# Joining values and scores of the first twelve attention trios, beginning the weights beside them, and spreading the later blocks

## The chip, the cores and the metric

The kernel runs on one core of a Trainium2 chip. The metric is the device time of one execution in microseconds (us); the profile of one execution gives the time of every instruction on the engines: TensorE (PE, matmuls; PEld its weight loads), VectorE (DVE), ScalarE (ACT), GpSimd (POOL) and SyncE (SP, which issues most DMAs).

## What is computed

Windowed attention over 8 batches and 8 heads of 576 positions (64 values a head), then a feed-forward layer on the 4608 x 512 result.

```python
scores = scale * np.matmul(q, k.transpose(0, 1, 3, 2))
mask_plain = (rel >= 0) & (rel < window)                                   # heads 0 to 3, window 32
mask_dil = (rel >= 0) & (rel < window * dilation) & (rel % dilation == 0)  # heads 4 to 7, dilation 4
attn = softmax(np.where(masks, scores, -1e9))
x = (attn @ v).transpose(0, 2, 1, 3).reshape(4608, 512)
h = x @ w_in                                   # 512 x 2048
g = h * np.clip(h + 3.0, 0.0, 6.0) / 6.0
out = g @ w_out                                # 2048 x 512
```

## The kernel before

**Attention.** The work is cut into 48 trios: a trio is one third of a batch's positions for four heads, in 12 query blocks of 32 positions and two pairs of heads. A trio's steps are: 24 small matmuls for the scores (`mm_scores`, 64 rows by 32 columns of the array each), softmax on VectorE and ScalarE (`softmax`: max L186, subtract L187, exp L191, and for later trios the mask added at L184), a turn of e (`st_turn_e`), 24 small matmuls for the values (`mm_values_first` or `mm_values`), the division by the row sums (`normalise`: z L198, reciprocal L199, x L201), a turn of x (`st_turn_x`), and the split of x into a rounded high part xh (ScalarE, L300) and the rest xl (GpSimd, L303). A small matmul of f32 data is two passes in the profile. The array has eight tiles of 64 x 32; scores use four of them, values four.

The first 12 trios (`NFIRST`) turn e and x on TensorE (`turn`, L243, with copies to SBUF on ScalarE at L246 and L248) and add their mask by a matmul (L215). The later ones turn by blocks on VectorE and by small DMAs (`turn_by_blocks`, L262 to L266), and their values of trio t and scores of trio t+1 are issued alternately as one block (`st_both`).

**Feed-forward.** The 4608 rows are cut into 12 chunks of 384. A step is a pair (chunk c, part f of 16). `gemm1` runs 12 matmuls of 384 columns into a PSUM buffer ps_h, of which there are two; each product is made of three, high by high, low by high and high by low part. ScalarE (L413, L417) and VectorE (L414, L418) make t, gh and gl of it; L414 frees ps_h. `gemm2` runs 9 matmuls of 512 columns into three ps_o buffers, two steps behind `gemm1`. Chunk 0 needs trios 0 to 4, chunk 1 also trios 5 to 9, and so on; chunk 3 needs trio 16.

**Weights.** Each of the 32 half parts of the weights is loaded as 64-bit words by one DMA (`load_w`) and converted in beats: `cv_fields` (ScalarE multiplies L339 and L340, VectorE shift L341), `cv_join` (VectorE and-or L347 and add L351, a custom instruction; ScalarE cast L352), `cv_split` (VectorE subtract L356). Part f needs half parts 2f and 2f+1.

**Order.** Each engine runs its instructions in a fixed order. A scheduler makes it from priorities that the program sets by `turn_of`, and from its own timeline. In the front, the first 15 rounds (tau), `first_items` gives the steps of the first trios; `LD`, `CB` and `EARLY` name the rounds in which a weight is loaded, a conversion beat is run, and a step of the feed-forward is begun; `BASE` and `CD` shift their priorities. `LEAD` steps of chunk 0 go ahead, then chunks 0 and 1 alternate. From chunk 2 on, the list `at` places the later attention blocks beside half steps (a step has two halves).

Of the kernel before, what the change touches and what calls it, by code (L numbers as in the profile page):

```python
# [8 lines left out]
F32 = mybir.dt.float32  # L9
# [9 lines left out]
P = 128  # L19
QB = 32  # L20
DIL = 4
RT = 3
TB = 4 * RT
SPARE = 2
WORK = 11
BEATS = 30  
CB = (6, 7, 8, 8, 10, 11)  
EXTRA = 2  
PRIO = -500
WARM = 8    # L30
ONV = ()
AHEAD = 1  
AHEAD0 = 2  
LD = (2, 3, 4, 6, 14)  
NFIRST = 12
FIRST0, FIRST1 = 5, 4
AT0, AT1 = 1, 8
NLOAD = 3
BASE = 13  
CD = 2    # L40
EARLY = (9, 11, 12, 12, 13)  
DEL = 0.2  
G2 = 0.8  
EV = -1.9  
NEG = -1.0e30


# [1 line left out]
def windowed_attention_ffn(ctx: ExitStack, tc: tile.TileContext, qk, vp, w, mask, out):  # L49
# [100 lines left out]
    def mm_scores(t, ps, i, u, r, masked):  # L150

        x, rows = kqs[t], slice(r * D, (r + 1) * D)
        n, kb, at = SLOTS * u + i, (SLOTS + 1) * u + i, QB * (2 * r + u)
        last["pe"] = nc.tensor.matmul(  # L154
            ps[at : at + QB, 2 * QB * i : 2 * QB * (i + 1)],
            lhsT=x[rows, KW + QB * n : KW + QB * (n + 1)], rhs=x[rows, QB * kb : QB * (kb + 2)],
            start=not masked, stop=(i == SLOTS - 1 or not masked),
        )

    def mm_values_first(t, ps, i, u, h):  # L160

        k, j = divmod(i, 2)
        rows, n, at, s = slice(j * D, (j + 1) * D), 4 * k + 2 * h + u, QB * (2 * u + j), 2 * k + h
        last["pe"] = nc.tensor.matmul(  # L164
            ps[at : at + QB, s * W : (s + 1) * W],
            lhsT=ats[t][rows, QB * n : QB * (n + 1)], rhs=vs[t][rows, n, :], start=True, stop=True,
        )

    def mm_values(t, ps, i, u, r):

        rows, n, at = slice(r * D, (r + 1) * D), SLOTS * u + i, QB * (2 * (1 - r) + u)
        last["pe"] = nc.tensor.matmul(  # L172
            ps[at : at + QB, i * W : (i + 1) * W],
            lhsT=ats[t][rows, QB * n : QB * (n + 1)], rhs=vs[t][rows, n, :], start=True, stop=True,
        )

    def softmax(t, ps, masked):
        e = work_tile("e")
        mx = small.tile([P, SLOTS], F32, name="mx")
# [6 lines left out]
        nc.vector.tensor_reduce(out=mx, in_=sv, axis=AX.X, op=ALU.max)  # L186
        nc.vector.tensor_tensor(  # L187
            out=ev, in0=sv, in1=mx.rearrange("p (s o) -> p s o", o=1).broadcast_to([P, SLOTS, 2 * QB]),
            op=ALU.subtract,
        )  # L190
        nc.scalar.activation(e, e, AF.Exp, scale=SCALE)  # L191
        es[t] = e
        load_qk(t + NLOAD)

    def normalise(t, ps):
        pv = ps[:, : SLOTS * W].rearrange("p (s x) -> p s x", x=W)
        z = small.tile([P, SLOTS], F32, name="z")
        nc.vector.tensor_scalar_add(z, pv[:, :, D], 1e-9)  # L198
        nc.vector.reciprocal(z, z)  # L199
        x = work_tile("x")  # L200
        nc.vector.tensor_tensor(  # L201
            out=x.rearrange("p (s x) -> p s x", x=D), in0=pv[:, :, 0:D],
            in1=z.rearrange("p (s o) -> p s o", o=1).broadcast_to([P, SLOTS, D]),
            op=ALU.mult,
        )
# [6 lines left out]
    def st_scores_first(t):  # L212
        ps = ps_a.tile([P, 512], F32, name="ps_a")
        _, kind, part = trios[t]
        nc.tensor.matmul(ps[:, :CH], lhsT=ident_b, rhs=mask_sb[:, 3 * kind + part], start=True, stop=False)  # L215
        for i, u, r in blocks():
            mm_scores(t, ps, i, u, r, True)
        softmax(t, ps, True)

    def st_values_first(t):  # L220
        ps = ps_a.tile([P, 512], F32, name="ps_a")
        for i, u, r in blocks():
            mm_values_first(t, ps, i, u, r)
        normalise(t, ps)

    def st_both(ts, tv):

        ps = ps_a.tile([P, 512], F32, name="ps_a") if ts is not None else None
        pv = ps_a.tile([P, 512], F32, name="ps_a") if tv is not None else None
        for i, u, r in blocks():  # L230
            if tv is not None:
                mm_values(tv, pv, i, u, r)
            if ts is not None:
                mm_scores(ts, ps, i, u, r, False)
        if tv is not None:
            normalise(tv, pv)
        if ts is not None:
            softmax(ts, ps, False)

    def turn(src, name):  # L240
        ps = ps_a.tile([P, 512], F32, name="ps_a")
        for r in range(RT):
            nc.tensor.transpose(ps[:, r * P : (r + 1) * P], src[:, r * P : (r + 1) * P], ident)  # L243
        dst = work_tile(name)
        if name == "a":
            nc.scalar.copy(dst, ps[:, :CH])  # L246
        else:
            nc.scalar.copy(  # L248
                dst.rearrange("p (u k x) -> p k u x", u=2, k=RT),
                ps[:, :CH].rearrange("p (k u x) -> p k u x", u=2, k=RT),  # L250
            )
        return dst

# [117 lines left out]
    def convert_beat():  # L371
        if beat["split"] < beat["join"]:
            cv_split(beat["split"])
            beat["split"] += 1
        if beat["join"] < beat["fields"]:
            cv_join(beat["join"])
            beat["join"] += 1
        p = beat["fields"]
        if p < NP:
            load_ahead(p + 1)  # L380
            if p < beat["loaded"]:
                cv_fields(p)
                beat["fields"] += 1
        load_ahead(p + (AHEAD if "g" in last else AHEAD0))

    def weights_ready(f):
        while beat["split"] < 2 * (f + 1):
# [74 lines left out]
    place = lambda p, step: beside.setdefault(halves[p], []).append(step)  # L462
    place(at[0] - FIRST1, lambda: st_both(NFIRST, None))
    place(at[0] - FIRST1 + 2, lambda: st_turn_e(NFIRST, turn_by_blocks))
    for i, p in enumerate(at):
        t = NFIRST + i
        more = t + 1 < T
        place(p, lambda t=t, more=more: st_both(t + 1 if more else None, t))
        place(p + 1, lambda t=t: st_turn_x(t, turn_by_blocks))
        if more:  # L470
            place(p + 2, lambda t=t: st_turn_e(t + 1, turn_by_blocks))
        place(p + 3, lambda t=t: st_split(t))

    def step_at(n):
        c, f = steps[n] if n < len(steps) else (None, None)
        turn_of(n)
# [12 lines left out]
        for step in beside.get((c, f, 1), []):  # L489
            step()  # L490
        turn_of(n + 0.9)
        if n < BEATS and n % EXTRA == 0:
            convert_beat()

    first[0] = BASE * STEP
# [8 lines left out]
    n = 0  # L504
    for tau in range(NFIRST + 3):
        turn_of(tau - BASE)
        for step, t in first_items(tau):
            step(t)
        turn_of(tau - BASE + CD)
        load_ahead(LD.count(tau) + beat["loaded"])  # L510
# [100 lines left out]
```

## Time and profile before

| | us |
|---|---|
| median of 3 runs | 922.7 |
| fastest run | 922.14 |
| the profiled execution | 923.19 |
| its span, first to last instruction | 921.4 |
| mean granted TensorE clock | 0.988 |

The third of the runs, at 4496.82 us, is an outlier and is left out of the argument. The profile comes from one execution. An instruction's row has its start and duration, engine, line, operation, what it writes and reads, and in brackets how long the engine had been idle before it and what ended that. A window's row has busy times, not progress: a busy TensorE may be running at half clock, which the granted clock tells (1.00 is full speed).

### The profile page before, as it was taken

Reading aid. Unit: us, or ns where it says so; the run is one execution under the profiler, and the core shown is the slowest. Engines: PE = TensorE matmul, PEld = TensorE weight load, DVE = VectorE, ACT = ScalarE, POOL = GpSimd, SP = SyncE. Lnnn points to the kernel's source line nnn. Section 1 sums busy time; section 2 is a strip of 40 time slices with the busy share of each in tenths; the row PEclk is TensorE's granted clock in tenths of the full one; section 3 lists DMA queues with packets and bytes.
Section 4 is the critical chain, followed back from the end, with each engine's and each line's share of the span. In section 5 each row is a group of like instructions: output and inputs, shape, how many; then the busy total and the mean of one; then the engine's idle time right before and its main releaser. Section 6 shows DMA issues by size and latency. Waiting matters only on the chain.

```text
span 921.4 us, 20615 instructions
## 1 busy us (share of the span) xinstructions
PE 892.1 (97%) x8732; PEld 795.2 (86%) x8732; DVE 447.5 (49%) x934; ACT 348.1 (38%) x661; POOL 58.9 (6%) x77
## 2 busy tenths in 40 slices
PE   7789999999889999999999999999999999999997
PEld 4569999988778998989899888989988998899996
DVE  3778878534544544544454454445444444422221
ACT  3767666532224333234233333323333332322322
POOL 0211000000010000001000100000000010000000
PEclk9999999999899999999999999999999999999999
DMA  9756233023222212212222122112212210100000
GB/s 326 252 182 260 78 92 92 24 92 90 87 88 93 75 52 82 82 48 86 56 72 85 49 82 82 53 58 81 74 48 82 84 33 10 43 5 1 35 1 34
DMA packets 37676, 74.87 MB, mean 81 GB/s; under 512 B 7248, under 2 KB 16464, under 8 KB 37584
## 3 DMA queue, kind: packets, MB, share of 16 engines
q1 hardware_dynamic: 32400, 64.12, 21.8%
q10 hardware_dynamic: 5184, 9.44, 2.8%
q8 instruction: 68, 1.11, 0.5%
q14 instruction: 24, 0.20, 0.1%
HBM read 57.02 MB, written 9.44 MB: 72 GB/s over the span
## 4 chain that ended last, share of the span: by engine, by line
PE 93%; DVE 3%; DMA 2%; ACT 1%; issue 0%; SPq 0%; DVEq 0%
PE ps_o L429 15%; PE ps_h L408 15%; PE ps_h L409 14%; PE ps_h L410 14%; PE ps_o L430 14%; PE ps_o L431 14%; PE ps_a L172 3%; PE ps_a L154 2%; DMA st<-in_w 1%; DMA kq<-in_qk 1%; PE ps_a L243 1%; DVE x L201 1%; PE ps_a L164 1%; DVE st L347 1%; DMA mi<-in_mask 1%
## 5 line engine op out<-in xcount | busy, mean ns | idle before, releaser
L408 PE MATMUL ps_h<-xh,wt 128*128 128x384 f32 x768 | 261.3, 340 | 7.2 <-DVE t L414 7.2
L409 PE MATMUL ps_h<-xl,wt 128*128 128x384 f32 x768 | 260.3, 339 | 0.0
L410 PE MATMUL ps_h<-xh,wt 128*128 128x384 f32 x768 | 260.1, 339 | 0.0
L414 DVE SCALAR_TENSOR_TENSOR t<-t,ps_h 128x384 f32<-128x384 f32 x192 | 106.0, 552 | 297.7 <-ACT t L413 277.5
L429 PE MATMUL ps_o<-wt,gh 128*128 128x512 f32 x576 | 228.9, 398 | 0.0
L430 PE MATMUL ps_o<-wt,gh 128*128 128x512 f32 x576 | 225.4, 391 | 0.0
L431 PE MATMUL ps_o<-wt,gl 128*128 128x512 f32 x576 | 221.5, 391 | 0.0
L413 ACT ACTIVATE t<-ps_h,three 128x384 f32<-128x384 f32 x192 | 111.5, 581 | 246.7 <-PE ps_h L410 240.7
L408 PEld LDWEIGHTS ps_h<-xh,wt 128*128 128x128 f32 x768 | 145.4, 189 | 16.2 <-DVE t L414 8.9
L418 DVE TENSOR_TENSOR gl<-t,gh 128x384 fp32r<-128x384 f32 x192 | 107.3, 559 | 95.2 <-ACT gh L417 95.1
L409 PEld LDWEIGHTS ps_h<-xl,wt 128*128 128x128 f32 x768 | 145.6, 190 | 7.5
L417 ACT CAST gh<-t 128x384 fp32r<-128x384 f32 x192 | 98.4, 513 | 136.2 <-DVE t L414 131.9
L410 PEld LDWEIGHTS ps_h<-xh,wt 128*128 128x128 f32 x768 | 146.0, 190 | 0.2
L431 PEld LDWEIGHTS ps_o<-wt,gl 128*128 128x128 f32 x576 | 108.2, 188 | 23.0
L429 PEld LDWEIGHTS ps_o<-wt,gh 128*128 128x128 f32 x576 | 109.1, 189 | 17.8
L430 PEld LDWEIGHTS ps_o<-wt,gh 128*128 128x128 f32 x576 | 108.9, 189 | 15.7
L303 POOL TENSOR_TENSOR xl<-xf,xh 128x384 fp32r<-128x384 f32 (+3 forms) x72 | 58.6, 825 | 752.2 <-ACT xh L300 751.5
L191 ACT ACTIVATE e<-e 128x384 f32<-128x384 f32 x48 | 25.2, 526 | 101.9 <-DVE e L187 101.7
L154 PE MATMUL ps_a<-kq 64*32 64x64 f32 x2304 | 54.6, 226 | 4.7 <-issue 3.6
L300 ACT CAST xh<-xf 128x384 fp32r<-128x384 f32 (+3 forms) x72 | 33.6, 533 | 48.9 <-DMA xf<-xf_t 48.7
L154 PEld LDWEIGHTS ps_a<-kq 64*32 64x32 f32 x2304 | 44.6, 107 | 8.7 <-issue 7.2
L172 PEld LDWEIGHTS ps_a<-v,a 64*32 64x32 f32 x1728 | 36.1, 105 | 10.7 <-issue 10.7
(41 smaller groups left out, 458.4 us busy)
## 6 DMA issues: line engine op xcount, KB each, us to landing
kq<-in_qk SPq DMA_DIRECT2D x48, 416.0 KB, 4.6
v<-in_v SPq DMA_DIRECT2D x48, 390.0 KB, 3.7
st<-in_w SPq DMA_DIRECT2D x32, 512.0 KB, 5.1
out<-o ACTq DMA_DIRECT2D x36, 256.0 KB, 2.1
a<-a_t SPq DMA_DIRECT2D x144, 24.0 KB, 1.8
xf<-xf_t SPq DMA_DIRECT2D x144, 24.0 KB, 1.8
mi<-in_mask SPq DMA_DIRECT2D x1, 608.0 KB, 4.6
```

The source lines that it names most:

```text
L154: last["pe"] = nc.tensor.matmul(ps[at : at + QB, 2 * QB * i : 2 * QB * (i + 1)], lhsT=x[rows, KW + QB * n : KW + QB * (n + 1)], rhs=x[rows ...
L172: last["pe"] = nc.tensor.matmul(ps[at : at + QB, i * W : (i + 1) * W], lhsT=ats[t][rows, QB * n : QB * (n + 1)], rhs=vs[t][rows, n, :], st ...
L408: nc.tensor.matmul(ph, lhsT=wt[f][:, 0, ks], rhs=a, start=(kt == 0), stop=False)
L409: nc.tensor.matmul(ph, lhsT=wt[f][:, 0, ks], rhs=b, start=False, stop=False)
L410: last["pe"] = nc.tensor.matmul(ph, lhsT=wt[f][:, 1, ks], rhs=a, start=False, stop=(kt == NK - 1))
L413: nc.scalar.activation(t, ph, AF.Relu, bias=three, scale=1.0)
L414: nc.vector.scalar_tensor_tensor(out=t, in0=t, scalar=6.0, in1=ph, op0=ALU.min, op1=ALU.mult)
L417: nc.scalar.copy(gh, t)
L418: nc.vector.tensor_tensor(out=gl, in0=t, in1=gh.bitcast(F32), op=ALU.subtract)
L429: nc.tensor.matmul(po[c][tt], lhsT=gh[:, ts], rhs=wt[f][:, 2], start=(f == 0), stop=False)
L430: nc.tensor.matmul(po[c][tt], lhsT=gh[:, ts], rhs=wt[f][:, 3], start=False, stop=False)
L431: last["pe"] = nc.tensor.matmul(po[c][tt], lhsT=gl[:, ts], rhs=wt[f][:, 2], start=False, stop=(f == NF - 1))
```

## The change

The first 12 trios go through `st_both` too: values of trio tau-2 and scores of trio tau are issued alternately, values on the four tiles that the scores leave free, so the array positions of both are exchanged. The turns of e (trio tau-1) and of x (trio tau-3) stand ahead of that block in a round. Weights are loaded one per round from round 2 and converted from round 4 on, one to two beats a round; the steps begin in round 8, when five trios are done, with four steps of chunk 0 ahead. The blocks of the later trios, from chunk 2 on, are 19/3 halves apart for the first ten and 8 halves after that (4 for the first six and 8 before), begin five halves before chunk 2, and split x one half later.

```diff
-CB = (6, 7, 8, 8, 10, 11)
-AHEAD = 1
-AHEAD0 = 2
-LD = (2, 3, 4, 6, 14)
-FIRST0, FIRST1 = 5, 4
-AT0, AT1 = 1, 8
-BASE = 13
-CD = 2
-EARLY = (9, 11, 12, 12, 13)
+AHEAD = 2
+LEAD = 4
+LD = (2, 3, 4, 5, 6, 7, 8, 9, 10, 11, 12, 13)
+CB = (4, 5, 6, 6, 7, 7, 8, 8, 9, 9, 10, 10, 11, 11)
+BASE = 8
+CD = 0.5
+EARLY = (8, 9, 10, 11, 12, 13, 13)
...
-    LEAD = 2
...
     def mm_scores(t, ps, i, u, r, masked):
-        n, kb, at = SLOTS * u + i, (SLOTS + 1) * u + i, QB * (2 * r + u)
+        h = r if t < NFIRST else 1 - r
+        n, kb, at = SLOTS * u + i, (SLOTS + 1) * u + i, QB * (2 * (1 - h) + u)
...
     def st_both(ts, tv):
+        masked = ts is not None and ts < NFIRST
+        if masked:
+            _, kind, part = trios[ts]
+            nc.tensor.matmul(ps[:, :CH], lhsT=ident_b, rhs=mask_sb[:, 3 * kind + part], start=True, stop=False)
         for i, u, r in blocks():
             if tv is not None:
-                mm_values(tv, pv, i, u, r)
+                (mm_values_first if tv < NFIRST else mm_values)(tv, pv, i, u, r)
             if ts is not None:
-                mm_scores(ts, ps, i, u, r, False)
+                mm_scores(ts, ps, i, u, r, masked)
...
     def first_items(tau):
-        todo = []
-        for lag, step in ((0, st_scores_first), (1, lambda t: st_turn_e(t, turn)), (2, st_values_first),
-                          (3, lambda t: st_turn_x(t, turn)), (3, st_split)):
-            if 0 <= tau - lag < NFIRST:
-                todo.append((step, tau - lag))
-        return todo
+        some = lambda t: t if 0 <= t < NFIRST else None
+        if some(tau - 1) is not None:
+            st_turn_e(tau - 1, turn)
+        if some(tau - 3) is not None:
+            st_turn_x(tau - 3, turn)
+            st_split(tau - 3)
+        if some(tau) is not None or some(tau - 2) is not None:
+            st_both(some(tau), some(tau - 2))
...
-    at = [FIRST0 + FIRST1 * i for i in range(6)]
-    at += [2 * NF * c + AT0 + AT1 * i for c in range(1, NCH) for i in range(4)]
-    at = at[: T - NFIRST]
+    at = [1 + 19 * i // 3 for i in range(10)]
+    at += [at[-1] + 8 * (i + 1) for i in range(T - NFIRST - 10)]
...
-        place(p + 3, lambda t=t: st_split(t))
+        place(p + 4, lambda t=t: st_split(t))
...
-        if n < BEATS:
+        if LEAD <= n < BEATS:
             convert_beat()
```

Further edits follow from these: the row positions in `mm_values_first`, the copy of the turned x (L248), and `load_ahead` at the head of a round.

What the scheduler makes of it is seen in the orders. Names with a number are single buffers. The first place is the front on TensorE, one round of the first trios; here the rows of the kernel before (L154 scores, L164 values, L243 turns, L215 mask).

```order
L215 MATMUL ps_a_252<-mi_78 128x384
L154 MATMUL ps_a_252<-kq_138 32x64 x24
L243 MATMUL ps_a_285<-ident_79,e_205 128x128 x3
L164 MATMUL ps_a_291<-v_103,a_216 32x65 x24
L243 MATMUL ps_a_323<-ident_79,x_246 128x128 x3
```

And of the changed kernel, from the end of one block to the beginning of the next (L151 scores, L161 values, L230 turns, L216 mask, L395 and L396 a piece of `gemm1`).

```order
L161 MATMUL ps_a_350<-v_105,a_258 32x65
L151 MATMUL ps_a_349<-kq_177 32x64
L395 MATMUL ps_h_803<-xh_76,wt_414 128x384
L396 MATMUL ps_h_803<-xl_77,wt_414 128x384
L230 MATMUL ps_a_420<-ident_79,e_407 128x128 x3
L230 MATMUL ps_a_426<-ident_79,x_403 128x128 x3
L216 LDWEIGHTS mi_78
L216 MATMUL ps_a_436<-mi_78 128x384
L161 MATMUL ps_a_437<-v_243,a_339 32x65
L151 MATMUL ps_a_436<-kq_250 32x64
```

Both turns and a piece of `gemm1` now stand between two blocks; before, the scores of a trio stood ahead of the turn of the trio before it. The second place is ScalarE in the same rounds: before (L191 exp, L339 and L340 multiplies, L246 and L248 copies of the turned e and x, L300 cast to xh).

```order
L246 COPY a_619<-ps_a_615 128x384
L191 ACTIVATE e_608<-e_608 128x384
L339 ACTIVATE st_331<-st_331 128x512
L340 ACTIVATE st_331<-st_331 128x512
L352 CAST wt_578<-st_331 128x512
L248 COPY xf_657<-ps_a_653 128x3x2x64
L300 CAST xh_76<-xf_657 128x2x48
L300 CAST xh_76<-xf_657 128x2x144
```

And in the changed kernel (L188 exp, L326 and L327 multiplies, L233 and L235 copies, L287 cast, L339 now the cast of a weight).

```order
L188 ACTIVATE e_407<-e_407 128x384
L233 COPY a_424<-ps_a_420 128x384
L235 COPY xf_430<-ps_a_426 128x6x2x32
L287 CAST xh_76<-xf_430 128x2x144
L287 CAST xh_76<-xf_430 128x2x48
L326 ACTIVATE st_252<-st_252 128x512
L327 ACTIVATE st_252<-st_252 128x512
L339 CAST wt_414<-st_252 128x512
```

The two multiplies have moved from behind exp to behind the casts of xh. The third place is VectorE at one of the first later blocks, before: TensorE has the whole groups ps_h_2638 and ps_h_2683 ahead of this block (ps_a_2574 its values).

```order
L414 SCALAR_TENSOR_TENSOR t_2555<-t_2555,ps_h_2542 128x384
L418 TENSOR_TENSOR gl_2559<-t_2555,gh_2558 128x384
L198 TENSOR_SCALAR z_2623<-ps_a_2574 128x6
L199 RECIPROCAL z_2623<-z_2623 128x6
L201 TENSOR_TENSOR x_2626<-ps_a_2574,z_2623 128x384
L184 TENSOR_TENSOR e_2630<-ps_a_2573,mi_78 128x384
L414 SCALAR_TENSOR_TENSOR t_2651<-t_2651,ps_h_2638 128x384
```

And in the changed kernel: TensorE has the whole group ps_h_2515 and eight of twelve matmuls of ps_h_2609 ahead of this block (ps_a_2545 its values).

```order
L401 SCALAR_TENSOR_TENSOR t_2528<-t_2528,ps_h_2515 128x384
L405 TENSOR_TENSOR gl_2532<-t_2528,gh_2531 128x384
L195 TENSOR_SCALAR z_2594<-ps_a_2545 128x6
L196 RECIPROCAL z_2594<-z_2594 128x6
L198 TENSOR_TENSOR x_2597<-ps_a_2545,z_2594 128x384
L181 TENSOR_TENSOR e_2601<-ps_a_2544,mi_78 128x384
L401 SCALAR_TENSOR_TENSOR t_2622<-t_2622,ps_h_2609 128x384
```

The multiplications of the groups that are complete on TensorE now stand ahead of the block's z.

More of the change, by code (lines that the diff above doesn't have):

```diff
@@ L162, in mm_values_first @@
         k, j = divmod(i, 2)
-        rows, n, at, s = slice(j * D, (j + 1) * D), 4 * k + 2 * h + u, QB * (2 * u + j), 2 * k + h
+        rows, n, at, s = slice(j * D, (j + 1) * D), 4 * k + 2 * (1 - h) + u, QB * (2 * j + u), 2 * k + h
         last["pe"] = nc.tensor.matmul(
             ps[at : at + QB, s * W : (s + 1) * W],
-            lhsT=ats[t][rows, QB * n : QB * (n + 1)], rhs=vs[t][rows, n, :], start=True, stop=True,
+            lhsT=ats[t][rows, QB * n : QB * (n + 1)], rhs=vs[t][rows, 4 * k + 2 * h + u, :], start=True, stop=True,
         )
@@ L210, in blocks @@
         return [(i, u, r) for i in range(SLOTS) for u in range(2) for r in range(2)]
[L212 to L224, printed above, removed]
     def st_both(ts, tv):
@@ L237, in st_both @@
         if ts is not None:
-            softmax(ts, ps, False)
+            softmax(ts, ps, masked)
     def turn(src, name):
@@ L248, in turn @@
             nc.scalar.copy(
[L249 to L250 removed]
+                dst.rearrange("p (u i x) -> p i u x", u=2, x=QB),
+                ps[:, :CH].rearrange("p (i u x) -> p i u x", u=2, x=QB),
             )
@@ L383, in convert_beat @@
                 beat["fields"] += 1
-        load_ahead(p + (AHEAD if "g" in last else AHEAD0))
+        load_ahead(p + AHEAD)
     def weights_ready(f):
@@ L458, in windowed_attention_ffn @@
     halves = [(c, f, k) for c in range(2, NCH) for f in range(NF) for k in range(2)]
-    at = [FIRST0 + FIRST1 * i for i in range(6)]
-    at += [2 * NF * c + AT0 + AT1 * i for c in range(1, NCH) for i in range(4)]
-    at = at[: T - NFIRST]
-    place = lambda p, step: beside.setdefault(halves[p], []).append(step)
-    place(at[0] - FIRST1, lambda: st_both(NFIRST, None))
-    place(at[0] - FIRST1 + 2, lambda: st_turn_e(NFIRST, turn_by_blocks))
+    at = [1 + 19 * i // 3 for i in range(10)]
+    at += [at[-1] + 8 * (i + 1) for i in range(T - NFIRST - 10)]
+    place = lambda p, step: beside.setdefault(halves[p] if p >= 0 else (1, NF + p // 2, p % 2), []).append(step)
+    place(-5, lambda: st_both(NFIRST, None))
+    place(-3, lambda: st_turn_e(NFIRST, turn_by_blocks))
     for i, p in enumerate(at):
@@ L491, in step_at @@
         turn_of(n + 0.9)
-        if n < BEATS and n % EXTRA == 0:
+        if LEAD <= n < BEATS and n % EXTRA == 0:
             convert_beat()
@@ L506, in windowed_attention_ffn @@
         turn_of(tau - BASE)
-        for step, t in first_items(tau):
-            step(t)
+        load_ahead(LD.count(tau) + beat["loaded"])
+        first_items(tau)
         turn_of(tau - BASE + CD)
-        load_ahead(LD.count(tau) + beat["loaded"])
         for _ in range(CB.count(tau)):
```

1 line of the change is left out of this document (removed).

## The prediction

> **What bounds the kernel now.** I read the page first (busy shares, the clock row), then a table of windows that cuts the span where TensorE begins and ceases to be unbroken, then the waits, and last the timelines of the two stretches where TensorE idles. In the table the columns are: window in us, busy time of each engine (instructions), granted TensorE clock, DMA share, GB/s.
>
> ```profile
> PE 892.1 (97%) x8732; PEld 795.2 (86%) x8732; DVE 447.5 (49%) x934; ACT 348.1 (38%) x661; POOL 58.9 (6%) x77
> ```
>
> ```profile
> 26.00:64.70 38.70, 27.48 (x657) 21.92 (x658) 29.00 (x62) 25.58 (x54) 8.41 (x11) 0.91 0.60 202
> 64.70:218.90 154.20, 154.20 (x962) 139.90 (x962) 103.79 (x192) 88.01 (x165) 6.22 (x7) 1.00 0.32 110
> 218.90:283.00 64.10, 56.89 (x747) 50.12 (x749) 31.12 (x74) 17.44 (x36) 6.13 (x8) 0.92 0.28 82
> 283.00:916.00 633.00, 633.00 (x5815) 569.81 (x5808) 272.69 (x581) 205.99 (x387) 35.84 (x45) 1.00 0.18 56
> ```
>
> TensorE is busy without a gap, at full clock, from 64.7 to 218.9 us and from 283 to 916 us. The change can win nothing there, since it removes no GEMM matmul and the later attention blocks keep their form. What can be won or lost lies in two places. One is the front, up to about 79 us, where TensorE waits for the attention of the first twelve trios and for the weights. The other is the stretch from 218.9 to 283 us, where it idles 64.10 - 56.89 = 7.2 us and has a clock of 0.92.
>
> **The stretch from 218.9 to 283 us.** First a row of the waits in it (us in total, times, longest), then rows of its ScalarE and VectorE timelines, then windows of one stall and of what follows it.
>
> ```profile
> PE ps_h L408 <- DVE t L414: 7.2, 5, 2.0
> ```
>
> ```profile
> 214.76 0.58 ACT L413 ACTIVATE t<-ps_h,three 128x384 f32<-128x384 f32 x1
> ```
>
> ```profile
> 220.17 0.17 DVE L198 TENSOR_SCALAR z<-ps_a 128x6 f32<-128x6 f32 x1 [7.26 <-PE ps_a L154]
> ...
> 221.53 0.54 DVE L414 SCALAR_TENSOR_TENSOR t<-t,ps_h 128x384 f32<-128x384 f32 x1
> ```
>
> ```profile
> 231.85:233.85 2.00, 0.04 (x1) 0.00 (x0) 1.87 (x6) 0.00 (x0) 0.00 (x0) 1.00 0.47 119
> 234.20:237.60 3.40, 3.40 (x13) 3.40 (x12) 3.02 (x8) 1.49 (x4) 0.00 (x0) 0.51 0.48 146
> ```
>
> The relu of a GEMM group is ready at 214.76 + 0.58 = 215.34 us, but VectorE multiplies it (L414) only at 221.53. In VectorE's order that L414 stands behind z of an attention block that TensorE has not yet run, and VectorE stands idle 7.26 us in front of z. A later GEMM group needs the PSUM buffer that L414 frees. TensorE stalls five times for that, 7.2 us together, and after a stall of 2.0 us its clock is 0.51 for 3.4 us. The clock lost in the stretch is 64.1 x 0.08 = 5.1 us. Together that is 12.3 us.
>
> In the changed program this L414 (its line is now L401) stands ahead of z, and the blocks come 6.3 half steps apart instead of 4. Counted through both old orders, the six blocks that follow the first one have one or two GEMM groups complete on TensorE whose L414 is still behind z on VectorE; the blocks eight halves apart have none, and the 633 us behind 283 have no TensorE idle time. No block of the changed program has a complete group behind z. I take the whole 12.3 us as won. Less would be won if idle time stays: the bound is nothing, if all five stalls only move.
>
> The Trainium skill (TensorE: Matmul & The Clock Gate, "HAM oscillation") asks only that gaps over about 3.4 us be avoided. By that the 2.0 us stalls would leave the clock alone, the term would be 7.2 instead of 12.3, and the sum 927. The row with 0.51 disagrees, and the row decides.
>
> What this could bring late is the split that a chunk waits for. The last trio of chunk 3 is now split at half 30, two halves ahead of that chunk; it had been at half 24. Its x is turned ahead of the next L414, so I cost this at nothing. Cover are the two GEMM steps in between, 4.1 us each by the pitches below. If the cover went, I estimate about 2 us at each of two chunks.
>
> **The front.** I measure it by a time minus the GEMM work that TensorE has done by then. The pitches come from the TensorE timeline: twelve matmuls of 384 columns start between 215.63 and 217.71 (0.173 us each), four of 512 columns between 217.71 and 218.62 (0.228 us each). The two windows count the matmuls of each kind, by the tile that they write (ps_h, then ps_o), up to 79.3 us, where the last turn of trio 11's x ends.
>
> ```profile
> 215.63 0.34 PE L408 MATMUL ps_h<-xh,wt 128*128 128x384 f32 x1
> ...
> 217.71 0.39 PE L429 MATMUL ps_o<-wt,gh 128*128 128x512 f32 x1
> ...
> 218.62 0.39 PE L430 MATMUL ps_o<-wt,gh 128*128 128x512 f32 x1
> ```
>
> ```profile
> 0.00:79.30 79.30, 13.66 (x72) 12.46 (x72) 2.73 (x5) 2.91 (x5) 0.94 0.72 252
> ...
> 0.00:79.30 79.30, 6.99 (x28) 5.25 (x29) 0.00 (x0) 0.94 0.72 252
> ```
>
> Before: 72 x 0.173 + 28 x 0.228 = 18.9 us of GEMM by 79.3 us, so the front costs 60.4 us. In the changed order that last turn has 84 + 45 such matmuls ahead of it, 24.8 us. The front is even if the turn ends at 85.2 us.
>
> When does it end? In the old order TensorE issues the scores of the next trio before it turns e of the last one. In the new order it turns e of trio n, then x of trio n-2, and only then runs the block with the scores of n+1. So trio n+1 cannot begin until the softmax of n is through VectorE and ScalarE: the rounds no longer overlap. ScalarE, moreover, has the two multiplies of the weight conversion (L339, L340; now L326, L327) behind exp, both copies and the casts of xh, where it had them right behind exp. VectorE's shift (L341, now L328) waits for them ahead of z. The durations come from an old round, by engine: VectorE, ScalarE, TensorE, and a row of windows for one later block of scores and values together (96 passes).
>
> ```profile
> 28.43 0.43 DVE L341 TENSOR_SCALAR st<-st 128x512 uint32<-128x512 uint32 x1 [1.15 <-ACT st L339]
> 28.89 0.69 DVE L347 SCALAR_TENSOR_TENSOR st<-st 128x512 uint32<-128x512 uint32 x1
> 29.50 0.16 DVE L198 TENSOR_SCALAR z<-ps_a 128x6 f32<-128x6 f32 x1
> 29.72 0.69 DVE L351 CUSTOM_DVE_ANT_0 st<-st 128x1024 uint16<-128x1024 uint16 x1
> 30.33 0.18 DVE L199 RECIPROCAL z<-z 128x6 f32<-128x6 f32 x1
> 30.55 0.56 DVE L201 TENSOR_TENSOR x<-ps_a,z 128x384 f32<-128x384 f32 x1
> 31.10 0.69 DVE L356 TENSOR_TENSOR wt<-st,wt 128x512 fp32r<-128x512 f32 x1
> 31.71 0.55 DVE L186 TENSOR_REDUCE mx<-ps_a 128x6 f32<-128x384 f32 x1
> 32.29 0.56 DVE L187 TENSOR_TENSOR e<-ps_a,mx 128x384 f32<-128x384 f32 x1
> ```
>
> ```profile
> 30.97 0.47 ACT L248 COPY xf<-ps_a 128x384 f32<-128x384 f32 x1
> 31.48 0.88 ACT L300 CAST xh<-xf 128x192 fp32r<-128x192 f32 x2
> 32.15 0.52 ACT L246 COPY a<-ps_a 128x384 f32<-128x384 f32 x1
> 32.88 0.52 ACT L191 ACTIVATE e<-e 128x384 f32<-128x384 f32 x1 [0.21 <-DVE e L187]
> 33.31 0.64 ACT L339 ACTIVATE st<-st 128x512 f32<-128x512 f32 x1
> ```
>
> ```profile
> 24.86 0.33 PE L215 MATMUL ps_a<-mi 128*128 128x384 bf16 x1
> 25.12 0.87 PE L154 MATMUL ps_a<-kq 64*32 64x64 f32 x48
> 25.92 0.55 PE L243 MATMUL ps_a<-ident,e 128*128 128x128 f32 x3
> ```
>
> ```profile
> 218.90:220.10 1.20, 1.16 (x96) 1.05 (x96) 0.00 (x0) 0.00 (x0) 1.00 0.00 0
> ```
>
> On VectorE I count distances from start to start: shift 0.46, and-or 0.61, z 0.22, add (L351) 0.61, reciprocal 0.22, x 0.55, low part (L356) 0.61, max 0.58, e 0.56; 0.55 each for L414 and its partner L418.
>
> Trio 1's scores now stand behind the first turn, where trio 2's stood, so its e is done when that of trio 2 was, at 11.56 us (row below). A round without weights is exp 0.52, two turns 1.10, mask 0.33, the block 1.16, then z, max, reciprocal, x and e, 2.13: 5.2 us for trio 3, and 0.55 less for trio 2, which has no x to turn yet. That brings 21.4 us.
>
> ```profile
> 11.00 0.56 DVE L187 TENSOR_TENSOR e<-ps_a,mx 128x384 f32<-128x384 f32 x1
> ```
>
> A round with one conversion (trios 4 and 5) is paced by the other way: exp 0.52, turn 0.55, copies 0.52 and 0.51, casts 0.67, multiply 0.64, shift 0.46, and-or 0.61, then z to e with the add, 2.74: 7.2 us. The block is hidden beside ScalarE's part of this. Two of them bring 35.8 us. In trios 6 to 11 there are two conversions, and the second shift and and-or lie between z and e: 1.07 us more, 8.3 us a round, 85.6 us after six. Behind the last e stand 22 VectorE instructions up to x of trio 11, 11.1 us by the same distances, and the turn, 0.55: 97.2 us. Minus 24.8, the front costs 72.4 us, 12.0 more than before.
>
> The merged block saves TensorE time: scores alone took 0.87 us and values alone as many passes, a block 1.16, so ten blocks save about 6 us. I cost that at nothing, because it is won where TensorE waits in any case. I also keep DMA out of the path: its share was 0.60 from 26 to 64.7 us, and the new rounds are longer with one weight or two each.
>
> **Sum.** The span is 921.4 us, the profiled execution 923.19. Minus 12.3, plus 12.0: 922.9. The median of the three runs, 922.7, is 0.5 below the profiled execution, so 922.
>
> **The rivals.** First, VectorE alone paces the front, with ScalarE's multiplies always ready. From the first shift to x of trio 11 it has 120 instructions, 61.1 us by the same distances: 21.4 + 61.1 + 0.6 = 83.1 us, a front of 58.3, 2.1 less than before, and a time of 908. For it: VectorE is busy 29.0 of 38.7 us from 26 to 64.7 already. Against it: in the old round, where the way to the multiplies is shorter, it still waits 1.15 us for them. 905 is the low end, if TensorE's saving counts too.
>
> Second, slower than before: the clock in the front. A new round has some 3 us of attention work for TensorE in 7 or 8 us. If every burst runs at half clock, this turn from an early slow spell prices it:
>
> ```profile
> 20.95 0.90 PE L243 MATMUL ps_a<-ident,x 128*128 128x128 f32 x3
> ```
>
> A turn takes 0.90 instead of 0.55 us, 1.6 times as long. Eight rounds lose two turns, 0.7 us each; two rounds lose block and mask as well, 1.6 us each; the first unbroken spell loses half of 3.4 us. That is 10.5 us, and a time of 932. It decides where a burst follows 2 us and more of waiting, as at 234.2 us above; the GEMM pieces put between (2, 4 and 2 matmuls in the first rounds that have any) hardly fill that. With one further wait in each round it would be about 940. The Trainium skill (TensorE: Matmul & The Clock Gate, "The HAM clock gate") has the clock halved after an idle window of about 3.4 us; here 2.0 us have been enough, which makes this rival likelier than by the page.
>
> Third, the spread does less than I think: L414 is free, but the closer split or the attention's small DMAs hold GEMM groups up. Then the 12.3 us come back in half or in whole, 928 to 934.
>
> **Chances and range.** My forecast 0.45, VectorE-paced 0.22, the clock 0.25, the rear 0.08. The range from 906 to 937 takes in the first rival but for its lowest end, and the second but for its highest. A measurement of this kernel tells about 2% from no change, so the bounds are 904 and 941: faster by more 0.05, within 0.87, slower by more 0.08.
>
> **What would show it.** No TensorE wait for L401 after 200 us, and a clock of 1.00 there. In the front, about 5, 7 and 8 us from one e subtraction to the next, the first multiply beginning behind the casts of xh, and the last turn of x at 97 us. I am wrong if that turn ends before 90 or after 105 us, or if TensorE still idles in the rear.

## The result, and the profile after

The changed kernel takes 927.84 us (median of 8 runs, 927.08 to 929.16), the kernel before 924.71 us beside it (median of 8 runs, of which one, 4496.82, lies far off). The ratio is 1.0038, with an interval of 1.0022 to 1.0054: a little slower, by more than the interval, where the forecast was no change. Without the one execution far off, the median before is 924.06 us. The profiled execution takes 928.6 us, 5.4 more than the one before, with a span of 926.8 us.

First the engines' line of the page, then the windows (us in the window, busy time of TensorE, its weight loads, VectorE, ScalarE and GpSimd with their instructions, granted clock, DMA share, GB/s), then the waits of TensorE up to 110 us (total, times, longest), the first two of the changed kernel, the third of the kernel before.

```profile
PE 890.5 (96%) x8732; PEld 794.4 (86%) x8732; DVE 444.6 (48%) x934; ACT 348.6 (38%) x661; POOL 58.8 (6%) x77
```

```profile
26.00:64.70 38.70, 23.36 (x539) 18.41 (x539) 24.28 (x51) 23.45 (x46) 6.31 (x8) 0.69 0.57 190
...
218.90:283.00 64.10, 64.10 (x685) 57.67 (x684) 32.60 (x73) 21.97 (x43) 6.16 (x8) 1.00 0.27 81
```

```profile
PE ps_a L230 <- ACT e L188: 22.4, 10, 5.2
PE ps_h L395 <- ACT wt L339: 6.0, 2, 3.4
```

```profile
PE ps_a L243 <- ACT e L191: 5.6, 4, 3.9
```

The rear stretch, 218.9 to 283 us, is without a gap and at full clock, as forecast: it had 56.89 us of work and a clock of 0.92. The front has become worse than forecast. TensorE works 23.36 of the 38.7 us from 26 to 64.7, at a clock of 0.69 where it was 0.91. Up to 110 us it now waits ten times for ScalarE's exp of e, 22.4 us together, where it waited four times, 5.6 us. That is the chain without overlap: each trio waits for the softmax of the last. The two waits of the GEMM pieces for a weight's cast, 6.0 us, delayed no turn: the exp that the turn behind them needs ended at 33.44 us, and the turn began at 33.50; behind the other the turn still waited 0.49 us for its exp.

How much the front costs is measured as in the prediction, by the matmuls written to ps_h and to ps_o up to the end of the last turn of x (the row of TensorE's timeline).

```profile
0.00:105.20 105.20, 18.93 (x85) 0.85 0.65 219
...
0.00:105.20 105.20, 11.19 (x45) 0.85 0.65 219
```

```profile
104.72 0.49 PE L230 MATMUL ps_a<-ident,x 128*128 128x128 f32 x3
```

85 x 0.173 + 45 x 0.228 = 25.0 us of GEMM by 105.2 us: the front costs 80.2 us, 19.8 more than before, where 12.0 more was forecast. The profiled execution lost 5.4, so everything behind the front gained 19.8 - 5.4 = 14.4, where 12.3 was forecast. Each front here and below is that of one profiled execution.

Where the front went over is seen in VectorE's timeline, by the subtractions that end the softmax of trios 1, 3, 5 and 11, and one shift:

```profile
13.47 0.56 DVE L184 TENSOR_TENSOR e<-ps_a,mx 128x384 f32<-128x384 f32 x1
...
25.23 0.55 DVE L184 TENSOR_TENSOR e<-ps_a,mx 128x384 f32<-128x384 f32 x1
...
36.97 0.66 DVE L328 TENSOR_SCALAR st<-st 128x512 uint32<-128x512 uint32 x1 [3.48 <-ACT st L326]
...
40.29 0.55 DVE L184 TENSOR_TENSOR e<-ps_a,mx 128x384 f32<-128x384 f32 x1
...
91.16 0.54 DVE L184 TENSOR_TENSOR e<-ps_a,mx 128x384 f32<-128x384 f32 x1
```

They end at 14.0, 25.8, 40.8 and 91.7 us; the forecast had 11.6, 21.4, 35.8 and 85.6. Trio 1 is 2.5 us late, trio 3 4.4, trio 5 5.0, trio 11 6.1, and the last turn 8.0. At 105.2 us it lies just beyond the 105 that the prediction named as a sign of being wrong. The clock of the same time: windows around one stall, then mask matmuls, the first scores and turns in TensorE's timeline.

```profile
38.20:41.40 3.20, 0.03 (x1) 0.00 (x0) 3.10 (x8) 1.14 (x2) 0.00 (x0) 0.87 0.79 254
41.40:54.20 12.80, 8.87 (x209) 6.92 (x209) 7.08 (x15) 8.47 (x18) 2.72 (x4) 0.50 0.34 108
```

```profile
6.39 0.50 PE L216 MATMUL ps_a<-mi 128*128 128x384 bf16 x1 [1.48 <-DMA mi<-in_mask]
6.82 1.50 PE L151 MATMUL ps_a<-kq 64*32 64x64 f32 x48
...
10.15 0.90 PE L230 MATMUL ps_a<-ident,e 128*128 128x128 f32 x3 [1.83 <-ACT e L188]
...
41.45 0.90 PE L230 MATMUL ps_a<-ident,e 128*128 128x128 f32 x3 [3.22 <-ACT e L188]
...
42.78 0.52 PE L216 MATMUL ps_a<-mi 128*128 128x384 bf16 x1
```

A stall of 3.2 us is followed by 12.8 us at a clock of 0.50, though TensorE works 8.87 of them; a second stall, of 3.39 us, lies among them. Turns take 0.90 us instead of 0.55, the mask 0.52 instead of 0.33. The turn at 10.15 us is slow too, and so are the first scores, 1.50 us instead of 0.87: in the changed kernel the clock is low in the first rounds already. The granted clock of the window from 0 to 26 us reads 1.00 all the same; here the durations tell more than the clock row. The theory from here on (A): the rear gains what the sum said, the front loses what the sum said, and the half clock adds some 8 us. The rivals are named with each run.

### The profile page after: what moved, and what is told of

It reads as the page before. It is cut to its first block, busy times and chain, and to the rows that moved or that the text cites. A ratio compares the mean times of both kernels' runs of the same rounds, so it can differ in the third digit from the quotient of the medians.

```text
span 926.8 us, 20647 instructions
## 1 busy us (share of the span) xinstructions
PE 890.5 (96%) x8732; PEld 794.4 (86%) x8732; DVE 444.6 (48%) x934; ACT 348.6 (38%) x661; POOL 58.8 (6%) x77
## 4 chain that ended last, share of the span: by engine, by line
PE 91%; DVE 4%; ACT 2%; DMA 1%; issue 1%; SPq 0%; DVEq 0%
PE ps_o L416 15%; PE ps_h L395 14%; PE ps_h L396 14%; PE ps_h L397 14%; PE ps_o L417 14%; PE ps_o L418 14%; PE ps_a L169 3%; PE ps_a L151 2%; PE ps_a L230 1%; DVE st L338 1%; DVE st L334 1%; DVE e L184 1%; DMA mi<-in_mask 1%; DMA st<-in_w 1%; PE ps_a L161 1%
## 5 line engine op out<-in xcount | busy, mean ns | idle before, releaser
L395 PE MATMUL ps_h<-xh,wt 128*128 128x384 f32 x768 | 261.0, 340 | 6.0 <-ACT wt L339 6.0
L401 DVE SCALAR_TENSOR_TENSOR t<-t,ps_h 128x384 f32<-128x384 f32 x192 | 106.2, 553 | 320.3 <-ACT t L400 309.5
L396 PE MATMUL ps_h<-xl,wt 128*128 128x384 f32 x768 | 258.9, 337 | 0.0
L395 PEld LDWEIGHTS ps_h<-xh,wt 128*128 128x128 f32 x768 | 144.8, 189 | 14.8 <-ACT wt L339 6.5
L396 PEld LDWEIGHTS ps_h<-xl,wt 128*128 128x128 f32 x768 | 144.8, 188 | 7.6
L188 ACT ACTIVATE e<-e 128x384 f32<-128x384 f32 x48 | 25.2, 525 | 125.4 <-DVE e L184 125.4
L151 PE MATMUL ps_a<-kq 64*32 64x64 f32 x2304 | 62.5, 241 | 0.0
L151 PEld LDWEIGHTS ps_a<-kq 64*32 64x32 f32 x2304 | 51.8, 114 | 1.5 <-issue 1.1
L287 ACT CAST xh<-xf 128x384 fp32r<-128x384 f32 (+3 forms) x72 | 33.7, 534 | 35.1 <-DMA xf<-xf_t 34.8
```

The lines of the kernel that those rows point to most:

```text
L151: last["pe"] = nc.tensor.matmul(ps[at : at + QB, 2 * QB * i : 2 * QB * (i + 1)], lhsT=x[rows, KW + QB * n : KW + QB * (n + 1)], rhs=x[rows ...
L395: nc.tensor.matmul(ph, lhsT=wt[f][:, 0, ks], rhs=a, start=(kt == 0), stop=False)
L396: nc.tensor.matmul(ph, lhsT=wt[f][:, 0, ks], rhs=b, start=False, stop=False)
L401: nc.vector.scalar_tensor_tensor(out=t, in0=t, scalar=6.0, in1=ph, op0=ALU.min, op1=ALU.mult)
```

## The experiments

All seven kernels compute the whole output. Times are medians. The first four ran beside a kernel before of 923.29 us (16 runs), the last three beside one of 923.38 us (13 runs).

### The rear alone

The kernel before, with the new placement of the blocks behind trio 12.

```diff
-    at = [FIRST0 + FIRST1 * i for i in range(6)]
-    at += [2 * NF * c + AT0 + AT1 * i for c in range(1, NCH) for i in range(4)]
-    at = at[: T - NFIRST]
+    at = [1 + 19 * i // 3 for i in range(10)]
+    at += [at[-1] + 8 * (i + 1) for i in range(T - NFIRST - 10)]
...
-        place(p + 3, lambda t=t: st_split(t))
+        place(p + 4, lambda t=t: st_split(t))
```

> The kernel before with the new places of the later blocks alone (the list of places and the later split), front as before. Theory A, the two parts of the change add up: 14 us less than before, about 910.5, no TensorE wait for L414 from 200 us on and a clock of 1.00 there. Rival B, the rear gains only because the new front has converted more weights by then: half of it at most, 917 or more, with stalls left.

Measured: 910.1 us (4 runs), ratio 0.9853 (0.9837 to 0.987). Its windows:

```profile
26.00:64.70 38.70, 29.08 (x654) 22.96 (x654) 27.05 (x57) 24.44 (x50) 8.18 (x10) 0.81 0.58 188
...
218.90:283.00 64.10, 64.10 (x684) 57.55 (x684) 32.72 (x73) 22.19 (x45) 6.47 (x8) 1.00 0.28 83
```

And its last turn of x, with windows up to the end of that turn, first of the kernel before, then of this one:

```profile
82.42 0.49 PE L243 MATMUL ps_a<-ident,x 128*128 128x128 f32 x3
```

```profile
0.00:79.30 79.30, 62.09 (x1344) 48.42 (x1345) 52.39 (x111) 46.37 (x94) 14.58 (x22) 0.94 0.72 252
0.00:82.90 82.90, 65.09 (x1344) 51.04 (x1345) 52.49 (x111) 46.70 (x94) 14.67 (x22) 0.88 0.70 240
```

The spread takes away all stalls of the stretch and its half clock, and is worth 13.2 us by itself, as theory A had it (910.5). Rival B, that the rear gains only behind the new front, is refuted. The old front varies from one execution to the next: up to that turn the engines ran the same instructions in the same order as in the kernel before, yet it ended at 82.9 us instead of 79.3, a front of 64.0 instead of 60.4 (72 and 28 GEMM matmuls, as before). TensorE's 1344 instructions were busy 3.0 us longer at the lower clock, 0.88 against 0.94; the idle time differs by 0.6. So the lower clock cost some 3 us with work and order unchanged. The profiled execution took 912.98 us, the most of the four.

### The front alone

The changed kernel with the old list of places, the reverse of the diff above.

> The changed kernel with the old places of the later blocks, new front alone. Theory A: 20 us more than before, about 944, five stalls of 7 us together and a clock of 0.92 in the rear as before. Rival B: 938 or less, since part of the stalls stays away.

Measured: 943.57 us (4 runs), ratio 1.0215 (1.02 to 1.023). Its windows:

```profile
218.90:283.00 64.10, 57.28 (x720) 50.43 (x719) 30.09 (x72) 16.38 (x33) 4.75 (x6) 0.95 0.30 86
283.00:400.00 117.00, 113.80 (x1200) 101.74 (x1199) 55.18 (x121) 39.35 (x76) 8.54 (x11) 1.00 0.25 76
```

With the new front alone the kernel is 20.3 us slower, as theory A had it; rival B (938 or less) is refuted. The two parts add up to +7.1, the whole change measured +3.1 by medians: the old rear stalls 6.8 + 3.2 = 10.0 us behind the new front, part of it now beyond 283 us, where it stalled 7.2 in all and not beyond 283 before. Five of the stalls are again waits for the relu's multiply (L403), 8.8 us together and 2.0 at most. With these 2.8 us the two sums agree within 2.

### Useless work against the half clock

The changed kernel with matmuls of a mask behind the first eight blocks, into a PSUM buffer that nobody reads, so that TensorE does not idle while VectorE and ScalarE do the softmax.

```diff
+FILL = (6, 6, 10, 10, 16, 16, 16, 8, 0, 0, 0, 0)
...
+        if masked and FILL[ts]:
+            warm = ps_a.tile([P, 512], F32, name="ps_a")
+            for _ in range(FILL[ts]):
+                nc.tensor.matmul(warm[:, :CH], lhsT=ident_b, rhs=mask_sb[:, 0], start=True, stop=True)
```

> The changed kernel with 6 to 16 mask matmuls of no use behind each of the first eight blocks, written to a PSUM buffer that nobody reads, only to keep TensorE's clock up while it waits; the orders are otherwise those of the changed kernel. If half clock makes the front 8 us longer than the sum of instructions: the front (time minus GEMM work) falls from 80 to about 73 us and the time to about 921, clock about 0.95 in the first 65 us. Rival, the clock is covered by the waits for ScalarE and VectorE: front 78 or more, time 926 or more.

Measured: 921.61 us (10 runs, 921.11 to 922.21), ratio to the kernel before 0.9979 (0.9969 to 0.9988), 6.2 us less than the changed kernel by medians and 5.4 by the two ratios to the kernel before. A window, the counts of matmuls, the timelines of VectorE and TensorE:

```profile
26.00:64.70 38.70, 28.09 (x596) 21.36 (x594) 29.57 (x62) 25.95 (x51) 6.68 (x8) 0.91 0.58 195
```

```profile
0.00:97.00 97.00, 18.03 (x84) 0.96 0.71 241
...
0.00:97.00 97.00, 11.14 (x45) 0.96 0.71 241
```

```profile
11.24 0.56 DVE L185 TENSOR_TENSOR e<-ps_a,mx 128x384 f32<-128x384 f32 x1
...
20.52 0.55 DVE L185 TENSOR_TENSOR e<-ps_a,mx 128x384 f32<-128x384 f32 x1
...
34.42 0.55 DVE L185 TENSOR_TENSOR e<-ps_a,mx 128x384 f32<-128x384 f32 x1
...
38.45 0.89 DVE L333 TENSOR_SCALAR st<-st 128x512 uint32<-128x512 uint32 x1 [2.88 <-ACT st L331]
...
41.86 0.54 DVE L185 TENSOR_TENSOR e<-ps_a,mx 128x384 f32<-128x384 f32 x1
42.33 0.67 DVE L339 SCALAR_TENSOR_TENSOR st<-st 128x512 uint32<-128x512 uint32 x1
...
82.94 0.54 DVE L185 TENSOR_TENSOR e<-ps_a,mx 128x384 f32<-128x384 f32 x1
```

```profile
6.10 0.34 PE L217 MATMUL ps_a<-mi 128*128 128x384 bf16 x1 [1.18 <-DMA mi<-in_mask]
6.37 0.87 PE L152 MATMUL ps_a<-kq 64*32 64x64 f32 x48
...
96.49 0.49 PE L235 MATMUL ps_a<-ident,x 128*128 128x128 f32 x3
```

And two rows of the changed kernel's VectorE, the second and-or and the e subtraction of the same trio 6:

```profile
48.02 0.65 DVE L334 SCALAR_TENSOR_TENSOR st<-st 128x512 uint32<-128x512 uint32 x1
...
49.05 0.55 DVE L184 TENSOR_TENSOR e<-ps_a,mx 128x384 f32<-128x384 f32 x1
```

Trios 1, 3, 5 and 11 end their softmax at 11.8, 21.1, 35.0 and 83.5 us, the last turn at 97.0; the front costs 97.0 - 84 x 0.173 - 45 x 0.228 = 72.2 us. The prediction had 11.6, 21.4, 35.8, 85.6, 97.2 and 72.4. With the clock at 0.91 instead of 0.69 the front comes out as summed up, and the rival (78 or more, 926 or more) is refuted. The agreement at the end is in part luck: the rounds of trios 6 to 11 took 48.5 us where 49.8 had been summed, and from trio 11's softmax to the end of the last turn it was 13.5 where the sum had 11.7.

The fill takes 8.0 us off the front, 80.2 - 72.2, and 5.8 of them come up to trio 5 (40.8 against 35.0). They are not all the half clock. The mask arrived 0.3 us earlier in this execution. Nor did the orders stay those of the changed kernel, as the expectation has it: the scheduler, in whose timeline the useless matmuls count too, put VectorE's and-or behind z, and the second one of trios 6 and 7 behind e, after 41.86 instead of before 49.05. From the shift to e those two rounds then took 3.41 and 3.46 us instead of 4.13 and 4.10, 1.4 us less. That leaves some 6 us, an estimate by difference, for the half clock; the first 0.8 of them, in the first mask and scores, lie ahead of any useless matmul, where the clock happened to be full here and was not in the changed kernel. The shift of the conversion still waits for ScalarE's multiplies, 2.88 us, and holds z behind it: ScalarE's way seems to pace these rounds here too.

### ScalarE's multiplies ahead of exp

The changed kernel without the order that holds the two multiplies of a weight behind TensorE's work, so that ScalarE does them ahead of exp.

```diff
-        pace(nc.scalar.mul(v, hi_w, 2.0**-112))
-        pace(nc.scalar.mul(a.bitcast(U32), lo_w.bitcast(U32), 2.0**-29))
+        nc.scalar.mul(v, hi_w, 2.0**-112)
+        nc.scalar.mul(a.bitcast(U32), lo_w.bitcast(U32), 2.0**-29)
```

> The changed kernel without the rule that ties ScalarE's two weight multiplies to the latest matmul: they stand ahead of exp, and VectorE's part of the conversion lies between e and the next z. If ScalarE's late multiplies pace the rounds: rounds with one conversion fall from 7 to 8 us to about 5.5, those with two by 1 us or so, the front from 80 to about 72 us, time about 920. Rival, VectorE's or TensorE's own work paces them: front 78 or more, time 926 or more.

Measured: 925.84 us (7 runs), ratio 1.0032 (1.0019 to 1.0044). The last turn of x ends at 102.35 us with 84 + 45 GEMM matmuls ahead of it, a front of 77.6 us (the 78.7 in the expectation of the next run is too high). Its row, and two waits of TensorE up to 110 us:

```profile
101.83 0.52 PE L230 MATMUL ps_a<-ident,x 128*128 128x128 f32 x3 [0.26 <-DVE x L198]
```

```profile
PE ps_a L230 <- ACT e L188: 17.2, 7, 3.7
...
PE ps_h L395 <- DVE t L401: 9.5, 4, 4.7
```

The expectation of theory A (72 us, 920) missed. The rival's figures (78 or more, 926 or more) are nearly met, but they do not say what paces the rounds. The wait for e fell by 5.2 us, and 9.5 us of a wait appeared that the changed kernel has not in its front: GEMM matmuls for the relu's multiply, which VectorE does behind the softmax, with the whole conversion now ahead of that. I took the clock for the other half of it, and put both edits together.

### Both together

The useless matmuls and the free multiplies, the two diffs above.

> The changed kernel with both single edits together: useless matmuls behind the first eight blocks, which nobody reads, and ScalarE's two multiplies of the weight conversion free to stand ahead of exp. Nothing is left out. The first edit alone gave a front of 72.4 us, the second alone 78.7. Theory A (two ways of about 7 us run beside each other, TensorE's at half clock and ScalarE's to the multiplies, and each edit alone uncovers the other): together they give more than the sum of the two, rounds 4 and 5 of about 5.5 us, a front of 64 to 68 us, and a time of 913 to 917. Rival B (the multiplies never pace a round, and the clock is all): no gain beside the fill alone, front 71 to 73, time 920 to 922.

Measured: 921.33 us (10 runs, 917.69 to 923.72), ratio 0.9974 (0.9954 to 0.9993); nothing beside the fill alone. The executions differ by 6 us. The profiled one took 923.24 us, and TensorE waited 3.1 us in it for the mask, against 1.2 in the profile of the fill. In the order of time, rounds 4 and 5 on VectorE, then part of them on ScalarE and TensorE:

```profile
24.10 0.55 DVE L185 TENSOR_TENSOR e<-ps_a,mx 128x384 f32<-128x384 f32 x1
...
28.32 1.07 DVE L348 TENSOR_TENSOR wt<-st,wt 128x512 fp32r<-128x512 f32 x1 [1.55 <-ACT wt L344]
29.32 0.15 DVE L196 TENSOR_SCALAR z<-ps_a 128x6 f32<-128x6 f32 x1
...
31.14 0.55 DVE L185 TENSOR_TENSOR e<-ps_a,mx 128x384 f32<-128x384 f32 x1
...
37.91 0.55 DVE L185 TENSOR_TENSOR e<-ps_a,mx 128x384 f32<-128x384 f32 x1
```

```profile
27.25 0.51 ACT L292 CAST xh<-xf 128x384 fp32r<-128x384 f32 x1
27.67 1.14 ACT L344 CAST wt<-st 128x512 fp32r<-128x512 f32 x2
```

```profile
32.30 0.55 PE L235 MATMUL ps_a<-ident,e 128*128 128x128 f32 x3 [0.40 <-ACT e L189]
```

The turn takes 0.55 us, so the clock is full here, and rounds 4 and 5 still take 7.0 and 6.8 us, where theory A wanted 5.5. It is not the clock that holds these two rounds, then. The shift no longer waits, but the next stage does: the cast of the weight (L344) stands on ScalarE where the multiplies stood, behind the copies and the cast of xh, and the low part (L348), which waits 1.55 us for it, has moved ahead of z on VectorE. The edit moved the wait two instructions down the same conversion. In the later rounds the wait of the run before stays: up to 110 us GEMM matmuls wait 8.3 us for the relu's multiply, against 0.2 in the fill alone. The measured time agrees with rival B, but B's reason, that the multiplies never pace a round, does not follow. What a round would take without any conversion wait ahead of z wasn't tried.

### The block ahead of the turn

The changed kernel with the block of scores and values ahead of the turns of e and x, so that the scores of the next trio need not wait for the softmax of this one.

```diff
+        if some(tau) is not None or some(tau - 2) is not None:
+            st_both(some(tau), some(tau - 2))
         if some(tau - 1) is not None:
             st_turn_e(tau - 1, turn)
...
-        if some(tau) is not None or some(tau - 2) is not None:
-            st_both(some(tau), some(tau - 2))
```

> The changed kernel with the order within a front round turned round: the block with the scores of trio n+1 stands ahead of the turn of e of trio n, so the scores need not wait for the softmax before them, and the rounds overlap again. Nothing is left out. Theory A (the front's loss comes from rounds that no longer overlap, made longer by the half clock that the waiting brings): the front, 80.3 us in the changed kernel, comes back to 60 to 68 us, the last turn of x ends by 93 us, and the time is 908 to 916. Rival B (the loss is the half clock alone, whatever the order, since attention work in short bursts is always separated by waits): the front stays at 76 us or more, and the time at 923 or more. Rival C (VectorE's conversions between z and e pace it, in either order): front about 70 to 74, time about 918 to 922.

Measured: 913.8 us (4 runs), ratio 0.9898 (0.9869 to 0.9926). A window, the counts, and the last turn:

```profile
26.00:64.70 38.70, 29.91 (x556) 22.24 (x545) 32.16 (x69) 28.68 (x59) 6.65 (x9) 0.91 0.66 222
```

```profile
0.00:90.00 90.00, 21.42 (x84) 0.94 0.75 265
...
0.00:90.00 90.00, 13.00 (x45) 0.94 0.75 265
```

```profile
89.53 0.49 PE L230 MATMUL ps_a<-ident,x 128*128 128x128 f32 x3
```

The front costs 90.0 - 24.8 = 65.2 us, 15.0 less than in the changed kernel, with no work added: where the block stands carries 15.0 of the 19.8 us that the front lost. Theory A is met in the front, the last turn and the time; rivals B and C are refuted. The clock rose from 0.69 to 0.91 with it, but how the 15.0 divide into rounds that overlap again and half clock that stays away was not measured. VectorE is busy 32.16 us of the window, more than in any other kernel but one. The 4.8 us that are left over the old front are not taken apart.

### The rear, with useless work in the old front

The first experiment with a few mask matmuls behind the scores of trios 2 to 9.

```diff
+FILL = (0, 0, 4, 8, 4, 4, 4, 6, 6, 8, 0, 0)
...
+        if FILL[t]:
+            warm = ps_a.tile([P, 512], F32, name="ps_a")
+            for _ in range(FILL[t]):
+                nc.tensor.matmul(warm[:, :CH], lhsT=ident_b, rhs=mask_sb[:, 0], start=True, stop=True)
```

> The kernel before with the new placement of the later blocks alone (910.1 us, front 64.0) and a few useless matmuls, which nobody reads, behind the scores of trios 2 to 9 in its old front. Nothing is left out. Theory A (part of the old front's cost is half clock too: 0.91 from 26 to 64.7 us, 3.5 us): the front falls to 59 to 62 us and the time to 905 to 908. Rival B (in the old front the rounds overlap and the half clock lies beside waits for VectorE, so that more work on TensorE only costs): front 64 or more, time 910 or more.

Measured: 904.62 us (4 runs, 903.28 to 905.0), ratio 0.9791 (0.9758 to 0.9825), the fastest of all. A window and the last turn:

```profile
26.00:64.70 38.70, 33.40 (x753) 26.98 (x752) 32.48 (x69) 30.11 (x63) 10.46 (x14) 1.00 0.73 240
```

```profile
74.34 0.49 PE L248 MATMUL ps_a<-ident,x 128*128 128x128 f32 x3
```

With a clock of 1.00 the old front ends its last turn at 74.8 us, with the 18.9 us of GEMM that it had: 55.9 us, 4.5 less than in the kernel before and 8.1 less than in the profile of the rear alone; by the medians of the two kernels it is 5.5. Rival B is refuted, and the gain is larger than theory A had it (59 to 62). How much of it is the clock stays open: the useless matmuls also changed the scheduler's order, so that VectorE and ScalarE run the front in another order than in the rear alone. In one round, for instance, x (29.99 us) now stands ahead of the and-or (30.46), where the and-or (31.24) had stood ahead of x (32.89).

## Why the prediction was off

**The step that failed** is the front's term, +12.0, which measured +19.8, and in it the choice to make the rounds up of durations at full clock (turns of 0.55, a block of 1.16) and to leave the half clock to a rival. In the changed kernel the turns between the waits took up to 0.90 us and the first scores 1.50 instead of 0.87. Of the 8.0 us by which the last turn came late, 5.0 had come by the softmax of trio 5; 0.5 of these are the mask, which arrived at 6.39 us where the forecast's starting row had it at 5.85, and the rest go with the slow clock. Another 1.1 came in the six rounds after that, 50.9 us against 49.8, and 1.9 behind them, 13.5 against 11.7. The 1.9 are not the clock, for they are the same with the fill: there the sum itself was too short. That the front would lose, and by rounds that no longer overlap, was right; the fill, in which the clock was mostly full, came out at 72.2 us against 72.4, with two errors that cancel, and puts the half clock at some 6 us, where the rival had priced it at 10.5. With 7.8 more in the front and 13.2 instead of 12.3 for the rear, the sum for the profiled execution would be 929.8; it took 928.6.

**The rear** was right in mechanism: no TensorE wait for L401 there, a clock of 1.00, no TensorE idle time at the closer split. Its size was 14.4 us by difference of the two executions and 13.2 by the run of it alone, against 12.3. The stalls were 7.2; the rest must then be more than the 5.1 of the clock's mean. What the last 1 to 2 us are stays open.

**VectorE alone pacing the front** (908) was refuted: its front of 58 is 22 us from the measured one, and in the round to 40.29 VectorE stands idle 3.48 us for ScalarE. **The rear giving its gain back** was refuted by the rear alone. **ScalarE's way** through exp, copies and casts as the pace of a round with one conversion: with the clock up, two such rounds took 34.42 - 20.52 = 13.9 us, 6.95 each, against 7.2. Taking the multiplies off this way did not shorten it; the rows show the wait at the cast behind them, which is on it too. That the multiplies alone set the pace is refuted by this, and that the whole way sets it is seen in the waits but not shown by taking it away.

**DMA and the merged blocks at nothing**: the DMA share of the stretch from 26 to 64.7 is 0.57 after, against 0.60. The saved TensorE time brought nothing that could be seen, in a front that waits; no run shows it by itself.

By the Trainium skill (TensorE: Matmul & The Clock Gate, "A second HAM failure mode: psum-queue depth-cycling") short idle times between groups of matmuls, repeated often, made the clock oscillate between half and full in a kernel that cycles through PSUM banks. The trace agrees in part: bursts between waits of 0.5 to 5.2 us ran at 0.69 on average from 26 to 64.7 us, and the turns change between 0.55 and 0.90 us. Most of these waits are not short, though, so no run here shows that short ones alone do it. The row of 12.8 us at 0.50, with TensorE 69% busy, shows that the clock can also stay low over more than one burst.

## What to carry to other kernels

A software pipeline is kept by the order of the steps on the in-order engine: if the step that waits for the softmax stands ahead of the next scores, the rounds run one behind the other whatever the merging saves, and 15 us of the front hung on where one step stands here. Where a change turns unbroken work into bursts between waits, cost the bursts at the clock that such bursts have in the trace, as part of the forecast and not as a rival. A few useless matmuls in the gaps raised the clock here and even paid, but compare the orders before the gain is called the clock's: here the scheduler changed them too. Moving one operation of a chain ahead did nothing here while the next one of the chain stayed in the same queue.

## What was not expected of the hardware

Work that nobody needs made the kernel quicker, by 6.2 us in the new front and 5.5 in the old (910.1 to 904.6). The clock of the stretch from 26 to 64.7 us rose with it, from 0.69 to 0.91 and from 0.81 to 1.00; but the orders changed too, so not all of it is shown to be the clock's. What the clock does by itself is seen in the rear alone: the same order in the front, and a TensorE busy 3.0 us longer. The clock also varies between executions of one kernel: with the fill and the free multiplies, the three executions of 917.69 to 918.5 us had a mean clock of 0.996 to 0.998, and the seven of 920.5 to 923.72 us one of 0.990 to 0.994. And a stall need not be long: in the kernel before, the three stalls of 2.0 us, which end at 233.88, 247.12 and 260.35 us, were each followed by matmuls of 384 columns of 0.52 or 0.53 us instead of 0.34, while behind the stall of 0.86 us that ends at 222.13 they stayed at 0.34.
